# Attention and two MLPs in one kernel: result of attention kept in f32, P transposed in blocks of two chunks by two query tiles, new lags

## The chip, the cores and the metric

The kernel runs on one core of a Trainium2 chip. The metric is the device time of one execution in microseconds (us), as the median of several runs. The engines are TensorE (PE in the rows; PEld is its loading of weights), VectorE (DVE), ScalarE (ACT), GpSimd (POOL) and SyncE (SP), whose queue issues nearly all DMAs.

## The reference

Attention over 4 batches, 8 heads, 576 positions and a head size of 64, with rotary positions on q and k. Its output, 2304 rows of 512, goes through two MLPs in turn. All is float32.

```python
q_rot, k_rot = (rotate(q), rotate(k))
scores = np.matmul(q_rot, k_rot.transpose(0, 1, 3, 2)) / np.sqrt(D)
scores = scores - np.max(scores, axis=-1, keepdims=True)
attn = np.exp(scores)
attn = attn / (np.sum(attn, axis=-1, keepdims=True) + 1e-09)
x = np.matmul(attn, v).transpose(0, 2, 1, 3).reshape(B * S, H * D)
x = (1 / (1 + np.exp(-(x @ w_gate))) * (x @ w_val)) @ w_out      # d_ff 1536
h = x @ w2_in                                                    # d_ff 2048
out = (h * (1 / (1 + np.exp(-1.702 * h)))) @ w2_out
```

## The kernel before

The kernel has an attention stage and an MLP stage. Products that must be nearly exact in f32 are made from numbers split into a high part (the f32 rounded to the type fp32r) and a low part (the rest, rounded likewise): `split_mm` multiplies low by high, high by low and high by high into one PSUM bank.

**Attention.** Work goes by pairs of heads, 16 in all (4 batches x 4 pairs). Of a head's 576 positions 512 are laid out as 4 query tiles of 128 and 64 are a tail. Both tails of a pair share a tile, so a pair has nine score units (`NU`): unit u = 2j + h is query tile j of head h, and unit 8 holds both tails. For each unit TensorE makes the scores (`scores`, L295 and L296), VectorE takes the negated row maximum (L298), ScalarE the exponential with its row sum (`exps`, L313). `normalise` adds 1e-9 to the sums, takes reciprocals (L327, L328) and lets GpSimd scale P in SBUF (L331). P of a query tile (`P`, 128 x 1152 for both heads, 4 buffers) and of the tails (`Pt`, one buffer) is transposed on TensorE in pieces of 128 x 128 (`transpose_p`, L356, L363, L368): three chunks of one query tile go into one PSUM bank (tag `pt`, 3 buffers, which the transposes of q and k share), and one copy on ScalarE or VectorE (L343, L341) takes them to `PT` (one buffer for either half of the queries). `pv` multiplies V by PT (L386: one head in either half of the array's columns, tiles of 128x64; L383: both heads' tails of V in one zero-padded tile that fills the array). One half of a pair's queries (256 columns) and then the other (320) go through the same single PSUM bank (`ps_x`). The result is split at once into `xhl`, high part by ScalarE (L407), low part by VectorE out of PSUM (L409), which is the input of the first MLP.

For the pairs to come, x (q and k) is loaded (L167 to L179), rotated on GpSimd (`rope_mul`, L211, L215) and VectorE (`rope_add`, L219), transposed (`transpose_qk`, L234), split (L243, L244) and stacked by six DMAs on SP's queue (`stack`, L274).

**What sets the order.** The order is written out by hand: `slot(G)` issues, for unit G counted over all pairs, the scores of that unit and whatever is due by tables of lags. `PT` and `PV` give for each transpose step and each P·V step how many units behind the start of its pair it is issued; `ROPE_MUL`, `ROPE_ADD`, `ROPE_T`, `LOAD`, `LOAD_V` how many ahead. `steps` fixes the order in a slot. Every engine works off its own queue in that order, and waits where data or a buffer isn't ready. In pairs 3 to 8 the first weight chunk is loaded and decoded, one instruction per slot (`step_decode`).

**MLPs.** After the last slot the pools of the attention stage are closed and those of the MLP stage opened. Weights come in 14 chunks (6 and 8) of 256 hidden columns; for each chunk all five blocks of rows (four of 512, one of 256) go through `hidden` (L419, `psh`) and `out1` or `out2` (L419, `pso`).

Of the kernel before, what the change touches and what calls it, by code (L numbers as in the profile page):

```python
# [31 lines left out]
def attention_then_mlps(  # L32
# [35 lines left out]
    rp = rot.enter_context(tc.tile_pool(name="rope", bufs=1))  # L68
# [7 lines left out]

    xhl = {}

    def new_xhl(n):
        xhl[n] = big.tile([P, 2, KT, width[n]], F32R, tag=f"xhl{width[n]}", name=f"xhl{n}", bufs=width.count(width[n]))  # L80
# [220 lines left out]
    def exps(i, u):  # L301
# [4 lines left out]
        if h == 0:  # L306
            st[i]["P"][j] = (
                sp.tile([P, 2 * S], F32, tag="P", name="P", bufs=4)
                if j < MAINC
                else sp.tile([P, S], F32, tag="Pt", name="Pt", bufs=1)  # L310
            )
# [21 lines left out]
    PIECES = ((0, 2 * P), (2 * P, S - 2 * P))  # L333


    PT_DVE = ((2, 1), (2, 2), (3, 2), (4, 1))
    PT_DVE_FIRST = ((0, 0), (2, 2), (3, 2))
# [7 lines left out]
    def transpose_p(i, j, g):  # L345


        a = 0 if j < 2 else 1
        if (j, g) in ((0, 0), (2, 0)):
            st[i]["PT", a] = sp.tile([P, NCHK, PIECES[a][1]], F32, tag=f"PT{a}", name=f"PT{a}", bufs=1)  # L350
        PT = st[i]["PT", a]
        pt = st[i]["P"][j]
        ps = ps_t.tile([P, 512], F32, tag="pt", name="ps_p", bufs=3)
        if j < MAINC:
            for t in range(3):
                nc.tensor.transpose(  # L356
                    ps[:, t * P : (t + 1) * P], pt[:, (3 * g + t) * P : (3 * g + t + 1) * P], ident
                )
            jo = (j - 2 * a) * P
            dst = PT[:, 3 * g : 3 * g + 3, jo : jo + P]  # L360
            copy((j, g) in (PT_DVE if i else PT_DVE_FIRST), dst, ps[:, : 3 * P].rearrange("p (t c) -> p t c", t=3))
        elif g == 0:
            nc.tensor.transpose(ps[:TAIL, :P], pt[:, 0:TAIL], ident)  # L363
            for h in range(2):
                copy((j, g) in (PT_DVE if i else PT_DVE_FIRST), PT[h * TAIL : (h + 1) * TAIL, MAINC, 2 * P :], ps[:TAIL, h * TAIL : (h + 1) * TAIL])
        else:
            for t in range(MAINC):
                nc.tensor.transpose(ps[:, t * P : (t + 1) * P], pt[:, TAIL + t * P : TAIL + (t + 1) * P], ident)  # L368
            src = ps.rearrange("p (t h c) -> p h t c", t=MAINC, h=2)
            for h in range(2):  # L370
                t = h * (MAINC + 1)
                copy((j, g) in (PT_DVE if i else PT_DVE_FIRST), PT[:, t : t + MAINC, 2 * P :], src[:, h])

    def pv(i, a, ts):
# [28 lines left out]
        def split():  # L403
            for blk, o, c, w in parts:
                if blk not in xhl:
                    new_xhl(blk)
# [15 lines left out]

    mlp = {}
# [21 lines left out]
    acc = {}  # L445
# [16 lines left out]
    def new_acc(n):  # L462
        acc[n] = mlp["acc"].tile(
            [P, KT * width[n]], F32, tag=f"acc{width[n]}", name=f"acc{n}", bufs=width.count(width[n])
        )

    def out1(c, nchunk, W, n, g):
        if c == 0:
            new_acc(n)
# [3 lines left out]
        for e in range(KT):  # L473
# [7 lines left out]
            if c == nchunk - 1:  # L481
                nc.scalar.activation(xhl[n][:, 0, e, :], a, AF.Copy)
                nc.gpsimd.tensor_tensor(xhl[n][:, 1, e, :], a, f(xhl[n][:, 0, e, :]), ALU.subtract)

    def out2(c, nchunk, W, n, g):
        if c == 0:
            new_acc(n)
# [25 lines left out]
    PT_STEPS = [(j, g) for j in range(MAINC) for g in range(3)] + [(MAINC, 0), (MAINC, 1)]  # L513
# [6 lines left out]
    FILL = 2  # L520
    dec = []
# [21 lines left out]
    def step_normalise(G):  # L543
        for i in range(npairs):
            for j in range(MAINC + 1):
                if G == NU * i + min(2 * j + 2, NU):
                    normalise(i, j)
# [152 lines left out]
```

## Time and profile before

| | us |
|---|---|
| median of 3 runs | 1158.08 |
| lowest, highest | 1157.78, 1158.6 |
| span of the profiled execution | 1156.3 |
| TensorE busy in it | 1125.3 |
| VectorE busy | 753.4 |
| ScalarE busy | 425.7 |
| GpSimd busy | 324.3 |

The span runs from the first to the last instruction of the profiled execution; the profile gives no other time for it. A matmul's duration in the rows is that of one instruction, and matmuls overlap, so what one costs is read from the distance between the starts of two. The attention stage ends, and the MLP stage begins, at 314 us.

### The profile page before, as it was taken

The numbers are of one execution on the slowest core, as the hardware profiler recorded it, in microseconds if no ns is written. First come the engines' busy times: TensorE is split into PE (matmuls) and PEld (weight loads), VectorE is DVE, ScalarE is ACT, GpSimd is POOL, SyncE is SP. The second block draws the span as 40 slices with busy tenths as digits, with TensorE's granted clock in tenths as the row PEclk, the third lists the DMA queues.
The fourth block names the chain that finished last, engine by engine and source line by source line (L and its number), as shares of the span: only waits on it lengthen the run. The fifth ranks groups of instructions, "written<-read, shape, count | busy, mean of one in ns | idle before, by whom it ended". The sixth has DMA issues, their size and how long they took to land.

```text
span 1156.3 us, 16339 instructions
## 1 busy us (share of the span) xinstructions
PE 1125.3 (97%) x6032; PEld 926.1 (80%) x6032; DVE 753.4 (65%) x1467; ACT 425.7 (37%) x937; POOL 324.3 (28%) x335
## 2 busy tenths in 40 slices
PE   3999999999999999999999999999999999999998
PEld 2777777777688888888888888888888888888886
DVE  6788897776454655545555455666767776676744
ACT  3777777777521211221212122342222223232221
POOL 6778787764210100100101002430010010010100
PEclk9999999999999999999999999999999999999999
DMA  4555665544110111111111111111111111111014
GB/s 133 138 145 150 144 165 131 118 100 99 39 53 20 54 38 37 55 37 37 55 37 55 37 37 37 34 39 39 38 46 45 37 55 37 37 55 37 19 37 128
DMA packets 46063, 76.15 MB, mean 66 GB/s; under 512 B 11728, under 2 KB 24016, under 8 KB 45984
## 3 DMA queue, kind: packets, MB, share of 16 engines
q1 hardware_dynamic: 45696, 74.19, 23.9%
q8 instruction: 48, 0.79, 0.3%
q0 software_dynamic: 288, 0.92, 0.2%
q14 instruction: 31, 0.25, 0.1%
HBM read 50.46 MB, written 4.72 MB: 48 GB/s over the span
## 4 chain that ended last, share of the span: by engine, by line
PE 83%; DVE 6%; DMA 5%; SPq 3%; issue 1%; ACT 1%; POOL 0%; POOLq 0%; DVEq 0%; ACTq 0%
PE psh L419 43%; PE pso L419 30%; PE ps_x L386 3%; PE ps_p L356 2%; PE pss L295 2%; DVE xr L219 2%; PE pss L296 2%; DMA Zs<-X 1%; DVE nm L298 1%; DMA X<-Y 1%; SPq L179 1%; DVE Y L244 1%; DVE PT L341 1%; PE ps_x L383 1%; DMA x<-in_k_dram 1%
## 5 line engine op out<-in xcount | busy, mean ns | idle before, releaser
L419 PE MATMUL psh<-xhl,w_in 128*128 128x512 f32 (+1 forms) x2400 | 504.3, 368 | 0.0
L419 PEld LDWEIGHTS psh<-xhl,w_in 128*128 128x128 f32 x2400 | 419.5, 189 | 75.7
L433 ACT ACTIVATE sg<-psh 128x512 f32<-128x512 f32 (+1 forms) x140 | 77.7, 555 | 366.9 <-PE psh L419 366.2
L419 PE MATMUL pso<-w_out,g 128*128 128x512 f32 x864 | 202.4, 389 | 0.0
L435 DVE TENSOR_TENSOR gf<-psh,sg 128x512 f32<-128x512 f32 (+1 forms) x140 | 89.1, 636 | 158.1 <-PE psh L419 111.6
L419 PEld LDWEIGHTS pso<-w_out,g 128*128 128x128 f32 x864 | 161.7, 188 | 33.2
L436 ACT ACTIVATE g<-gf 128x512 fp32r<-128x512 f32 (+1 forms) x140 | 82.5, 589 | 242.5 <-DVE gf L435 242.5
L139 POOL TENSOR_TENSOR w_in<-wt,w_in 128x512 fp32r<-128x512 f32 x40 | 51.8, 1294 | 391.0 <-DVE w_in L138 391.0
L437 DVE TENSOR_TENSOR g<-gf,g 128x512 fp32r<-128x512 f32 (+1 forms) x140 | 95.3, 681 | 91.7 <-ACT g L436 91.7
L419 PE MATMUL pso<-g,w_out 128*128 128x512 f32 (+1 forms) x720 | 152.8, 368 | 0.0
L419 PEld LDWEIGHTS pso<-g,w_out 128*128 128x128 f32 x720 | 125.8, 189 | 22.6
L298 DVE TENSOR_REDUCE nm<-pss 128x1 f32<-128x576 f32 x144 | 107.8, 749 | 52.3 <-PE pss L296 51.2
L331 POOL TENSOR_SCALAR P<-P,r 128x576 f32<-128x576 f32 x128 | 103.9, 824 | 73.2 <-DVE r L328 25.8
L139 POOL TENSOR_TENSOR w_out<-wt,w_out 128x512 fp32r<-128x512 f32 x28 | 36.2, 1293 | 263.9 <-DVE w_out L138 263.9
L313 ACT ACTIVATE P<-pss,nm 128x576 f32<-128x576 f32 x128 | 95.5, 746 | 32.5 <-DVE nm L298 31.8
L495 DVE TENSOR_TENSOR acc<-pso,acc 128x512 f32<-128x512 f32 x126 | 83.2, 686 | 20.3 <-PE pso L419 18.0
L386 PE MATMUL ps_x<-PT,v 128*64 128x320 f32 (+1 forms) x512 | 79.3, 420 | 4.2 <-DVE xhl L409 4.2
L356 PE MATMUL ps_p<-ident,P 128*128 128x128 f32 x576 | 81.7, 273 | 0.9 <-POOL P L331 0.9
L480 DVE TENSOR_TENSOR acc<-pso,acc 128x512 f32<-128x512 f32 (+1 forms) x100 | 61.6, 635 | 28.7 <-PE pso L419 28.7
L343 ACT ACTIVATE PT<-ps_p 128x384 f32<-128x384 f32 (+2 forms) x178 | 71.5, 440 | 21.9 <-PE ps_p L356 21.2
L356 PEld LDWEIGHTS ps_p<-ident,P 128*128 128x128 f32 x576 | 67.9, 140 | 2.2 <-POOL P L331 1.4
L295 PE MATMUL pss<-X 128*128 128x288 f32 (+3 forms) x176 | 54.6, 337 | 1.1 <-ACT P L313 0.5
(62 smaller groups left out, 1034.5 us busy)
## 6 DMA issues: line engine op xcount, KB each, us to landing
raw<-in_moe_w_out_dram SPq DMA_DIRECT2D x28, 512.0 KB, 3.5
raw<-in_moe_w_in_dram SPq DMA_DIRECT2D x16, 512.0 KB, 3.7
raw<-in_moe_w_gate_dram SPq DMA_DIRECT2D x12, 512.0 KB, 3.9
raw<-in_moe_w_val_dram SPq DMA_DIRECT2D x12, 512.0 KB, 3.8
Z<-X SPq DMA_DIRECT2D x15, 288.0 KB, 3.0
Z<-Y SPq DMA_DIRECT2D x15, 288.0 KB, 3.2
X<-Y SPq DMA_DIRECT2D x15, 288.0 KB, 3.1
x<-in_q_dram SPq DMA_DIRECT2D x16, 256.0 KB, 3.1
```

What stands on the lines that cost most here:

```text
L139: lambda: nc.gpsimd.tensor_tensor(w[:, 1, :], f(t), f(w[:, 0, :]), ALU.subtract),
L295: nc.tensor.matmul(ps[:m, n, o : o + w], T[:, q0 : q0 + m], rhs, start=True, stop=False)
L298: nc.vector.tensor_reduce(nm, ps[:, :, :HALF], axis=AX.XY, op=ALU.max, negate=True)
L313: nc.scalar.activation(st[i]["P"][j][:, c : c + S].rearrange("p (n c) -> p n c", n=2), ps[:, :, :HALF], AF.Exp, bias=nm, accum_out=st[i][" ...
L331: nc.gpsimd.tensor_scalar(pt, pt, r[:, c - a : c - a + 1], 1.0, op0=ALU.mult, op1=ALU.mult)
L356: nc.tensor.transpose(ps[:, t * P : (t + 1) * P], pt[:, (3 * g + t) * P : (3 * g + t + 1) * P], ident)
L386: nc.tensor.matmul(ps[h * D : (h + 1) * D, :n], vt[:, h * MAINC + t, :], PT[:, h * (MAINC + 1) + t, :], start=(t == 0), stop=False,)
L419: nc.tensor.matmul(ps, l(sl, a), r(sr, a), start=(sl == 1 and a == 0), stop=(sl + sr == 0 and a == n - 1))
L435: nc.vector.tensor_tensor(gf, pss[-1][:, :wd], sg, ALU.mult)
L436: nc.scalar.activation(g[:, 0, m, :], gf, AF.Copy)
L437: nc.vector.tensor_tensor(g[:, 1, m, :], gf, f(g[:, 0, m, :]), ALU.subtract)
L495: nc.vector.tensor_tensor(a, ps[:, :DM], a, ALU.add)
```

## The change

- The result of P·V is copied to f32 tiles `xf` (ScalarE alone); it is split into `xhl` later, by `split_x`: block 0 at slot 144 + `DRAIN`, the other blocks in the first MLP chunk, one block ahead of `hidden`. `xf` and the accumulators `acc` share buffers; `xhl` lives in pools on the other side of SBUF that are opened where `rot` and `soft` are closed.
- A transpose step takes chunk t and chunk t + 5 of two query tiles: four transposes, one copy of 512 columns; chunk 4 gives two transposes and 256 columns. There are 12 steps per pair where there were 14. The first step of the tails transposes 128 columns of `Pt` where it took 64.
- `normalise` takes two query tiles at once: one add and one reciprocal for four columns. It now comes first in a slot, ahead of the scores.
- Buffers: `P` 5, `Pt` 2, `PT` 2 of each half.
- The lags and the order within a slot are new; which copies go to VectorE (`PT_DVE`) too. Pair 0 has no lags of its own.

```diff
-                nc.scalar.activation(xhl[blk][:, 0, hp, o : o + w], ps[:, c : c + w], AF.Copy)
-            for blk, o, c, w in parts:
-                nc.vector.tensor_tensor(
-                    xhl[blk][:, 1, hp, o : o + w], ps[:, c : c + w], f(xhl[blk][:, 0, hp, o : o + w]), ALU.subtract
-                )
+                at = hp * width[blk] + o
+                nc.scalar.activation(xf[blk][:, at : at + w], ps[:, c : c + w], AF.Copy)
...
+    def split_x(n, e, src, eng):
+        a = src.rearrange("p (e w) -> p e w", w=width[n])[:, e, :]
+        nc.scalar.activation(xhl[n][:, 0, e, :], a, AF.Copy)
+        eng.tensor_tensor(xhl[n][:, 1, e, :], a, f(xhl[n][:, 0, e, :]), ALU.subtract)
+    def split_block(n):
+        new_xhl(n)
+        for e in range(KT):
+            split_x(n, e, xf[n], nc.vector if e % 2 else nc.gpsimd)
...
-    def normalise(i, j):
+    def normalise(i, js):
         s = st[i]["sum"]
-        a = 2 * j
-        b_ = min(a + 2, 2 * MAINC + 1)
-        r = sp.tile([P, 2], F32, tag="r", name="r", bufs=4)[:, : b_ - a]
-        for c in range(a, b_):
-            nc.vector.tensor_scalar_add(r[:, c - a : c - a + 1], s[:, c : c + 1], 1e-9)
+        a = 2 * js[0]
+        b_ = min(2 * js[-1] + 2, NU)
+        r = sp.tile([P, 4], F32, tag="r", name="r", bufs=4)[:, : b_ - a]
+        nc.vector.tensor_scalar_add(r, s[:, a:b_], 1e-9)
         nc.vector.reciprocal(r, r)
         for c in range(a, b_):
-            pt = st[i]["P"][j][:, (c - a) * S : (c - a + 1) * S]
+            j, h = divmod(c, 2)
+            pt = st[i]["P"][j][:, h * S : (h + 1) * S]
             nc.gpsimd.tensor_scalar(pt, pt, r[:, c - a : c - a + 1], 1.0, op0=ALU.mult, op1=ALU.mult)
...
-    PT_DVE = ((2, 1), (2, 2), (3, 2), (4, 1))
+    QT = MAINC + 1
+    PT_DVE = (6, 11, 8, 1, 9, 7)
...
-        if j < MAINC:
-            for t in range(3):
-                nc.tensor.transpose(
-                    ps[:, t * P : (t + 1) * P], pt[:, (3 * g + t) * P : (3 * g + t + 1) * P], ident
-                )
+        if t < QT:
+            chs = (t, QT + t) if t < MAINC else (t,)
+            for x, c in enumerate(chs):
+                for y in range(2):
+                    nc.tensor.transpose(
+                        ps[:, (2 * x + y) * P : (2 * x + y + 1) * P],
+                        st[i]["P"][2 * a + y][:, c * P : (c + 1) * P],
+                        ident,
+                    )
+            dst = PT[:, t : chs[-1] + 1 : QT, : 2 * P]
+            copy(dve, dst, ps[:, : len(chs) * 2 * P].rearrange("p (t c) -> p t c", c=2 * P))
...
-    LOAD, LOAD_V, LOAD_VTAIL = 27, 13, 3
-    ROPE_MUL = {ANY: (20, 19, 16, 17, 18, 15), 1: (22, 20, 18, 14, 17, 14), 2: (22, 20, 17, 22, 18, 17)}
-    ROPE_ADD = {ANY: (15, 10), 1: (15, 14), 2: (13, 11)}
-    ROPE_T = {ANY: (8, 7, 6), 1: (9, 9, 7), 2: (10, 9, 7)}
-    PT = {ANY: (5, 6, 7, 7, 7, 9, 9, 11, 9, 10, 14, 13, 12, 13), 0: (5, 6, 8, 5, 7, 6, 7, 8, 9, 10, 13, 14, 14, 12), npairs - 1: (5, 9, 9, 6, 7, 11, 10, 11, 12, 12, 14, 12, 15, 13)}
+    LOAD, LOAD_V, LOAD_VTAIL = 27, 10, 5
+    ROPE_MUL = {ANY: (24, 20, 19, 18, 24, 13), 1: (21, 19, 19, 18, 19, 16), 2: (21, 19, 13, 20, 20, 19)}
+    ROPE_ADD = {ANY: (11, 10), 1: (16, 10), 2: (11, 12)}
+    ROPE_T = {ANY: (9, 7, 6), 1: (9, 7, 6), 2: (10, 7, 6)}
+    PT_STEPS = [(0, t) for t in range(QT)] + [(1, t) for t in range(QT + 2)]
+    PT = {ANY: (6, 6, 7, 9, 7, 10, 10, 13, 12, 12, 14, 14), npairs - 1: (7, 9, 10, 13, 7, 10, 14, 17, 17, 11, 17, 15)}
+    NORM = ((0, 1), (2, 3), (4,))
-    PV_EARLY = (0, 5, 6, 7, 8, 9)
-    PV = {ANY: (10, 10, 12, 13, 13, 15, 15, 17, 17, 17), 0: (8, 8, 9, 11, 12, 15, 15, 17, 17, 17), npairs - 1: (14, 16, 16, 16, 16, 19, 19, 20, 20, 20)}
+    PV_EARLY = (0,)
+    PV = {ANY: (11, 13, 13, 13, 14, 17, 17, 17, 17, 19), npairs - 1: (11, 16, 16, 16, 16, 21, 22, 22, 23, 23)}
...
-            steps = (step_scores, step_rope, step_decode, run_later, step_pt, step_load, step_pv_early, step_normalise, step_pv, step_exps)
+            steps = (step_normalise, step_scores, step_rope, step_pv, step_decode, step_pv_early, run_later, step_load, step_exps, step_pt)
...
+            if G == NU * npairs + DRAIN:
+                rot.close()
+                mlp["x", 0] = ctx.enter_context(tc.tile_pool(name="xhl_a", bufs=1, side="right", reuse_waits="tile"))
+                split_block(0)
...
+                if at == 0 and n + 1 < NBLK:
+                    split_block(n + 1)
                 g = hidden(kind, W, n)
```

## Rows read from the trace of the kernel before

**Rows 1.** The page: span; busy us (share) xinstructions; granted TensorE clock in 40 slices
```profile
span 1156.3 us, 16339 instructions
...
PE 1125.3 (97%) x6032; PEld 926.1 (80%) x6032; DVE 753.4 (65%) x1467; ACT 425.7 (37%) x937; POOL 324.3 (28%) x335
...
PEclk9999999999999999999999999999999999999999
```

**Rows 2.** Busy time by stretch: a decoding pair, a later pair (stretch, length, engines)
```profile
122.00:140.00 18.00, 17.66 (x131) 13.66 (x129) 15.80 (x42) 13.65 (x37) 15.03 (x17) 1.00 0.61 155
212.00:230.00 18.00, 17.62 (x130) 13.59 (x129) 13.58 (x37) 13.17 (x36) 12.95 (x16) 1.00 0.50 122
```

**Rows 3.** TensorE in order of time, one pair: start, length, line, tiles [idle before]
```profile
200.26 1.08 PE L386 MATMUL ps_x<-PT,v 128*64 128x256 f32 x8
201.27 0.40 PE L295 MATMUL pss<-X 128*128 128x288 f32 x1
201.51 0.30 PE L296 MATMUL pss<-X,Y 128*128 128x288 f32 x1
201.65 0.30 PE L295 MATMUL pss<-X 128*128 128x288 f32 x1
...
203.11 0.49 PE L234 MATMUL ps_qk<-ident,xr 128*128 128x128 f32 x3
203.68 0.27 PE L363 MATMUL ps_p<-ident,Pt 128*64 128x128 f32 x1
203.88 0.65 PE L386 MATMUL ps_x<-PT,v 128*64 128x256 f32 x4
204.46 0.40 PE L295 MATMUL pss<-X 128*128 128x288 f32 x1
...
209.58 1.30 PE L386 MATMUL ps_x<-PT,v 128*64 128x320 f32 x8 [0.29 <-DVE xhl L409]
...
216.01 1.14 PE L356 MATMUL ps_p<-ident,P 128*128 128x128 f32 x9
216.91 0.38 PE L295 MATMUL pss<-Z 128*128 128x288 f32 x1
...
219.29 0.40 PE L295 MATMUL pss<-X 128*128 128x288 f32 x1
```

**Rows 4.** Groups by line and shape: xcount | busy, mean ns | idle before
```profile
L433 ACT ACTIVATE sg<-psh 128x512 f32<-128x512 f32 x112 | 67.1, 599 | 306.4 <-PE psh L419 306.3
...
L493 DVE COPY acc<-pso 128x512 f32<-128x512 f32 x18 | 11.7, 685 | 1.7 <-PE pso L419 1.5
```

**Rows 5.** GpSimd and SP's queue in order of time, from 206 to 226
```profile
210.58 1.47 POOL L331 TENSOR_SCALAR P<-P,r 128x576 f32<-128x576 f32 x2 [0.47 <-DVE r L328]
...
222.53 1.97 POOL L331 TENSOR_SCALAR P<-P,r 128x576 f32<-128x576 f32 x2 [1.31 <-ACT PT L343]
...
214.96 0.39 SPq L187 DMA_DIRECT2D v<-in_v_dram  x1
...
218.71 0.59 SPq L179 DMA_DIRECT2D x<-in_k_dram  x1
```

**Rows 6.** DMA issues, 206 to 226: count, KB each, median us to landing
```profile
x<-in_k_dram SPq DMA_DIRECT2D x2, 16.0 KB, 2.4
```

**Rows 7.** TensorE in order of time, the fill and the start of pair 2
```profile
24.03 0.44 PE L295 MATMUL pss<-X 128*128 128x288 f32 x1
24.27 0.44 PE L296 MATMUL pss<-X,Y 128*128 128x288 f32 x1
...
28.75 0.40 PE L295 MATMUL pss<-Z 128*128 128x288 f32 x1 [0.92 <-ACT P L313]
...
53.08 0.54 PE L295 MATMUL pss<-X 128*128 128x288 f32 x1
```

**Rows 8.** TensorE in order of time, the drain and the first MLP matmul
```profile
311.37 2.38 PE L386 MATMUL ps_x<-PT,v 128*64 128x320 f32 x16 [0.93 <-DVE xhl L409]
...
314.07 6.31 PE L419 MATMUL psh<-xhl,w_in 128*128 128x512 f32 x26
```

More of the change, by code (lines that the diff above doesn't have):

```diff
@@ L67, in attention_then_mlps @@
     ps_t = soft.enter_context(tc.tile_pool(name="ps_t", bufs=1, space=PSUM))
-    rp = rot.enter_context(tc.tile_pool(name="rope", bufs=1))
+    rp = rot.enter_context(tc.tile_pool(name="rope", bufs=1, side="right"))
     ps_s = rot.enter_context(tc.tile_pool(name="ps_s", bufs=2, space=PSUM))
@@ L74, in attention_then_mlps, with new_f32 @@
     vtail = [sp.tile([P, P], F32, tag=f"vtail{n}", name=f"vtail{n}") for n in range(2)]
+    mlp = {}
     xhl = {}
+    xf = {}
+    acc = {}
     def new_xhl(n):
-        xhl[n] = big.tile([P, 2, KT, width[n]], F32R, tag=f"xhl{width[n]}", name=f"xhl{n}", bufs=width.count(width[n]))
+        xhl[n] = mlp["x", min(n, 1)].tile([P, 2, KT, width[n]], F32R, tag=f"xhl{n}", name=f"xhl{n}", bufs=1)
+    def new_f32(n, name):
+        return big.tile(
+            [P, KT * width[n]], F32, tag=f"f32_{width[n]}", name=f"{name}{n}", bufs=width.count(width[n])
+        )
[3 more added lines that the diff above has]
+        eng.tensor_tensor(xhl[n][:, 1, e, :], a, f(xhl[n][:, 0, e, :]), ALU.subtract)
     stage = [stage_a]
@@ L343, in copy, with transpose_p @@
             nc.scalar.activation(dst, src, AF.Copy)
[L345 to L350, printed above, removed]
+    def transpose_p(i, n):
+        a, t = PT_STEPS[n]
+        if ("PT", a) not in st[i]:
+            st[i]["PT", a] = sp.tile([P, 2 * QT - 1 + a, PIECES[a][1]], F32, tag=f"PT{a}", name=f"PT{a}", bufs=2)
         PT = st[i]["PT", a]
-        pt = st[i]["P"][j]
+        dve = n in (PT_DVE if i else PT_DVE_FIRST)
         ps = ps_t.tile([P, 512], F32, tag="pt", name="ps_p", bufs=3)
-        if j < MAINC:
-            for t in range(3):
-                nc.tensor.transpose(
-                    ps[:, t * P : (t + 1) * P], pt[:, (3 * g + t) * P : (3 * g + t + 1) * P], ident
-                )
[L359 to L363, printed above, removed]
+        if t < QT:
[6 more added lines that the diff above has]
+                        ident,
+                    )
+            dst = PT[:, t : chs[-1] + 1 : QT, : 2 * P]
+            copy(dve, dst, ps[:, : len(chs) * 2 * P].rearrange("p (t c) -> p t c", c=2 * P))
+            return
+        pt = st[i]["P"][MAINC]
+        if t == QT:
+            nc.tensor.transpose(ps[:, :P], pt[:, 0:P], ident)
             for h in range(2):
-                copy((j, g) in (PT_DVE if i else PT_DVE_FIRST), PT[h * TAIL : (h + 1) * TAIL, MAINC, 2 * P :], ps[:TAIL, h * TAIL : (h + 1) * TAIL])
+                copy(dve, PT[h * TAIL : (h + 1) * TAIL, MAINC, 2 * P :], ps[:TAIL, h * TAIL : (h + 1) * TAIL])
         else:
@@ L368, in transpose_p @@
                 nc.tensor.transpose(ps[:, t * P : (t + 1) * P], pt[:, TAIL + t * P : TAIL + (t + 1) * P], ident)
[L369 to L372, printed above, removed]
+            dst = PT.rearrange("p (h t) c -> p h t c", h=2)[:, :, :MAINC, 2 * P :]
+            copy(dve, dst, ps.rearrange("p (t h c) -> p h t c", t=MAINC, h=2))
     def pv(i, a, ts):
@@ L404, in split @@
             for blk, o, c, w in parts:
-                if blk not in xhl:
-                    new_xhl(blk)
-                nc.scalar.activation(xhl[blk][:, 0, hp, o : o + w], ps[:, c : c + w], AF.Copy)
-            for blk, o, c, w in parts:
-                nc.vector.tensor_tensor(
-                    xhl[blk][:, 1, hp, o : o + w], ps[:, c : c + w], f(xhl[blk][:, 0, hp, o : o + w]), ALU.subtract
-                )
+                if blk not in xf:
+                    xf[blk] = new_f32(blk, "xf")
+                at = hp * width[blk] + o
+                nc.scalar.activation(xf[blk][:, at : at + w], ps[:, c : c + w], AF.Copy)
         later.append(split)
@@ L443, in hidden @@
         return g
-    acc = {}
     row_runs = []
@@ L460, in attention_then_mlps @@
         row_runs.append(runs)
[L462 to L465, printed above, removed]
     def out1(c, nchunk, W, n, g):
         if c == 0:
-            new_acc(n)
+            acc[n] = new_f32(n, "acc")
         wd = width[n]
@@ L507, in attention_then_mlps @@
     ANY = None
[L508 to L514 removed]
+    LOAD, LOAD_V, LOAD_VTAIL = 27, 10, 5
[5 more added lines that the diff above has]
+    NORM = ((0, 1), (2, 3), (4,))
     PV_STEPS = [(a, [t]) for a in range(2) for t in range(MAINC + 1)]
[L516 to L517 removed]
+    PV_EARLY = (0,)
+    PV = {ANY: (11, 13, 13, 13, 14, 17, 17, 17, 17, 19), npairs - 1: (11, 16, 16, 16, 16, 21, 22, 22, 23, 23)}
     DEC_PAIR, DEC_UNIT = (3, 4)
     FILL = 2
+    DRAIN = 10
     dec = []
@@ L544, in step_normalise @@
         for i in range(npairs):
-            for j in range(MAINC + 1):
-                if G == NU * i + min(2 * j + 2, NU):
-                    normalise(i, j)
+            for js in NORM:
+                if G == NU * i + min(2 * js[-1] + 2, NU):
+                    normalise(i, js)
     def step_rope(G):
```

18 lines of the change are left out of this document (8 added, 10 removed).

## Prediction

> **What bounds the kernel now.** I read the page first: a span of 1156.3 us in which TensorE is busy 97% [rows 1]. That share does not say whether TensorE has anything to give, so the next views are the busy time by stretch and the start times of TensorE's instructions. Of 18 us in the middle of the attention stage TensorE is busy 17.6 while VectorE has 13.6, ScalarE 13.2 and GpSimd 13.0; in the pairs that also decode the first weight chunk the others rise to 15.8, 13.7 and 15.0 [rows 2]. The scores of one unit begin at 201.27 and those of the same unit of the next pair at 219.29 [rows 3]: a pair takes 18.02 us, and the 16 pairs some 288 of the 314 us before the first MLP matmul [rows 8]. The MLPs behind that are untouched but for the splitting of their input, so the question is what of the 18.02 us is work.
>
> Start-to-start differences give it [rows 3]. A score matmul of 288 columns takes 0.135 us (201.51 to 201.65). Nine transposes and the following first score take 0.90 + 0.22 (216.01, 216.91, and the next some 0.22 later), so one transpose takes 0.109. The group of eight P·V matmuls of 256 columns lasts 1.01 to the next score and the group of four 0.58, so one takes (1.01 - 0.58)/4 = 0.107 and, in proportion, 0.133 for 320 columns; the zero-padded tail of V, which fills the array, is twice that each. Per pair: 36 full score matmuls 4.8, the narrow tail unit 0.6, 41 + 9 transposes 5.45, P·V 2.15 + 2.67. That is 15.6 us. The other 2.4 us is what can move.
>
> Where it lies: a group of P·V matmuls (array tiles of 128x64) costs more than its matmuls. Eight of them: 1.01, then 0.24 to the second score instead of 0.135, less 8 x 0.107: 0.25 at the way out. On the way in, the four at 203.88 start 0.20 after a transpose of 0.11: 0.09. I take 0.35 per group; groups of four and of eight give the same, so it goes by group and not by matmul. A pair has five (200.26, 203.88, 209.58 and two more like them): 1.75. The 64-row transpose of the tail starts 0.57 after three transposes of 0.33 (203.11, 203.68): 0.24 lost, and the profile names no releaser; what ends then is the subtraction that frees the PSUM buffer taken three steps before. Last, 0.29 is lost at 209.58 to VectorE's subtraction of the attention result, which holds the one P·V bank. Sum 15.6 + 1.75 + 0.24 + 0.29 = 17.9 of 18.02.
>
> **The change, part by part.** I call the start of a pair's nine units T0, and a unit with all that is issued in it a slot; u is its number in the nine.
>
> Attention result kept in f32. The subtraction on VectorE goes; the one P·V bank is then freed by a single ScalarE copy. With the new lags the tail of the first half lies in u5 and the next use in u8; that of the second half in u1 and the next use in u2, behind score and q/k transposes: some 1.0 us later than the copy is done. The wait of 0.29 goes, and nothing is next in line there. The split returns as four ScalarE copies and four subtractions (two VectorE, two GpSimd) per block: for block 0 in the drain, where these engines have no other work, for the others one block ahead of TensorE in the first MLP chunk, where TensorE is the engine that is busy. I cost it at nothing; uncovered, block 0's chain would cost 4 x 0.6 us on ScalarE [rows 4] plus one subtraction, about 3.3 us, and the last P·V matmuls (3.0 us) and the first low-half matmuls lie over it. In the drain the present kernel waits 0.93 for the same subtraction [rows 8]; that goes too.
>
> New P·V lags. Per pair there are now three groups in 64-column tiles: one step in u2, three in u4, four in u8 directly behind the narrow scores; the two tails of V fill the array and stand alone. Two groups less at 0.35: 0.70 less. Bounds: 0 if the cost goes with something that stays, 0.9 if the way in behind scores (u4) is free as well.
>
> Transposes in twos. The number stays 41; the tail's first one is 128 wide, and moves to u5, where the buffer three steps back has long been copied: 0.24 less. Copies become wider and fewer: 512 columns cost VectorE 0.685 (the copy of an MLP output) and ScalarE 0.60 [rows 4]. VectorE gets five of 512 and one of 256 where it had three of 384 and two of 256, and loses the subtraction and most of nine tiny adds and five reciprocals: within 1 us of 13.6, hence no bound. ScalarE loses a little.
>
> So 0.29 + 0.70 + 0.24 = 1.23 us per pair on TensorE. Against it stand the waits that the trace of before doesn't show, and for these I laid the slots out by hand. TensorE's work in u0 to u8 becomes 1.3, 1.9, 1.6, 1.5, 2.6, 1.5, 1.4, 1.2 and 3.6. It is uneven: u5 to u7 are short, and there the chain score, maximum, exponential is longest against them. Two places come out tight.
>
> First, normalising two tiles at once. The new order puts it ahead of the scores, so VectorE's adds wait for the fourth unit's exponential and the maximum of u4 is queued behind them; u4 begins at T0 + 6.4, and VectorE has from u3, behind a maximum done at 6.1, a q/k split (0.5) and two PT copies (0.65, 0.4) left: to 7.8, with add and reciprocal 8.1. GpSimd then needs four pieces: 0.735 each as a rule, 0.98 where VectorE adds at the same time (two in 1.47 at 210.58, in 1.97 at 222.53 [rows 5]), so T0 + 11.05, and the first transpose step of u6, which reads all four pieces, is asked for at T0 + 11.04 (u6 begins at 10.5, its scores take 0.53). A wait of 0 to 0.2. Ahead of these pieces GpSimd has two rope products in u3 that wait for the new pair's x and for the q/k transposes that free their output. SP issues v at the end of u8 (214.96 before) and the last x piece 3.75 us later (218.71), which lands 2.4 after that [rows 5, 6]: T0 + 6.4; the products end at T0 + 7.5, ahead of 8.1. It just fits.
>
> Second, the three transpose buffers in u7: the fifth step of that run needs the first one's buffer, whose ScalarE copy is queued behind the exponential of u6: maximum to 11.75, exponential to 12.6, copy to 13.15, and TensorE asks at 12.9. About 0.25 of wait. Together I take 0.35 per pair, between 0 and 1.0. Gain 1.23 - 0.35 = 0.88.
>
> The six pairs that decode: one extra VectorE instruction per slot delays nothing on these two chains by my layout, as they run from u5 to u1, and u8 is long. Queues: the stacking DMAs leave in the same slot as before, and v's and x's issue still waits for the last P·V step with v.
>
> Fill. In the first slots TensorE waits for the exponentials (0.92 at 28.75) [rows 7]. P is transposed from unit 6 instead of 5, later steps too; the four pieces are there at about 32.1, the tail unit begins at 34.15; pair 1's q/k come a slot later, and the stacking DMAs then end about 1 us after unit 9 asks, which by my layout begins at 36.4. One pair's slots, 16.65, then put pair 2 at 53.05; before it is 53.08 [rows 7]. But 0.64 us more of work is then outstanding (the second half's tail of V, 0.53, and one transpose).
>
> TensorE's clock in the fill: two scores at 24.03 and 24.27 stand 0.24 us apart [rows 7], 288 columns at the lower level, 1.2 GHz, though the granted clock of that slice reads 9 tenths or more [rows 1]; before that it had mostly waited. In the steady state it is 0.135, the 2.4 level; a first score lasts 0.40 there (201.27) and again at 28.75, against 0.44 at 24.03, so the rate has risen by then, in a stretch full of waits. The Trainium skill (TensorE: Matmul & The Clock Gate, "Part 1: The HAM clock gate") says that low is the default and that activity lifts it. By that rule the thinner slots 1 to 5 could stay at the lower rate. Read from rows alone: five slots x 4 scores x 0.105 = 2.1 us, 2.7 with the q/k transposes, if none of it hides under the exponentials; I put this among the rivals.
>
> Sum: 14 pairs x 0.88 = 12.3, the drain 0.93, the fill 0.03 - 0.64: 12.6 us. The profiled span of 1156.3 becomes 1143.7. The profile gives no time for that execution beside its span; the median of the runs, 1158.1, is 1.8 longer. Adding this, 1145.5.
>
> **The rivals.** No new wait: GpSimd at 0.735 a piece and small reserves where I counted none. 14 x 1.23 + 0.3 = 17.5: 1140.6. For it: the engines other than TensorE have 4 to 5 us free per pair [rows 2].
>
> The P·V cost doesn't go by group (it is paid at each turn between f32 and scores, or the tails of V alone in a slot pay it): 14 x (0.53 - 0.35) + 0.3 = 2.8: 1155.3. For it: no row shows P·V directly behind full-width scores, or a tail of V between scores and transposes.
>
> The fill stays at the lower rate: 1145.5 + 2.7 = 1148.2.
>
> Slower: the new wait on GpSimd outgrows the gain. If x lands 1.5 us later (the lag of the first product behind the load shrinks from seven slots to three), the products end at T0 + 8.7, and with pieces of 0.98 the normalising ends at 12.6: 1.6 us of wait before u6, 1.85 with the second place, against 1.23. 14 x -0.62 + 0.3 = -8.4: 1166.5. It decides from an end of the four pieces at about T0 + 12.1, 1 us later than I work out. Against it: measured landings of x are near 2.4 and the late start would come only with DMA queues fuller than now.
>
> **How the numbers follow.** Forecast 45%, no new wait 18%, cost not by group 14%, slow fill 12%, late normalising 11%. The range takes in all but the last: 1139 to 1157. About 0.2% (2.3 us) is what a measurement of this kernel tells from no change. Faster: the first, second and fourth, and over half of the third, 0.83; same 0.08; slower 0.09.
>
> **What would show it.** A period near 17.15 us from score to score of two pairs; three groups of 128x64 P·V per pair; no wait of P·V for VectorE; a wait of transposes for GpSimd's P of at most 0.2 us and one on a PSUM buffer of about 0.25; pair 2 near 53; the first MLP matmul near 301.5 with no gap. I am wrong if the period stays near 18 (then a new wait stands in u6 or u7, or the group cost is not one), or if the MLP stage itself changes length.

## Result and the profile after

The changed kernel takes 1166.74 us (1166.07 to 1168.45), the kernel before 1158.23 beside it: a ratio of 1.0075, 95% interval 1.0060 to 1.0089. It is slower by 8.5 us; 1145.5 was forecast, and 1157 was the end of the range. The page of the changed kernel, to set beside [rows 1]:

```profile
span 1164.8 us, 15987 instructions
...
PE 1132.9 (97%) x6032; PEld 924.4 (79%) x6032; DVE 779.1 (67%) x1316; ACT 415.9 (36%) x894; POOL 341.4 (29%) x345
...
PEclk9999999999999999999999999999999999999999
```

The instructions of TensorE are as many as before, the granted clock is the same, and TensorE is busy 7.6 us longer. Where that lies is told by four moments in TensorE's order of time, which both kernels have. Attention is divided where the narrow scores of unit 8 start, in pair 1 and in pair 15.

| from ... to | before | after | difference |
|---|---|---|---|
| start to pair 1's narrow scores | 50.77 | 51.96 | +1.2 |
| pair 1's to pair 15's, 14 periods | 250.0 | 241.8 | -8.2 |
| to the first MLP matmul | 13.3 | 13.0 | -0.3 |
| to the end of the span | 842.2 | 858.0 | +15.8 |
| span | 1156.3 | 1164.8 | +8.5 |

So attention became 7.3 us shorter, which has the sign of the forecast, and the MLPs, which were to stay as they were, 15.8 us longer. I take the four parts in the order of their size.

**The MLPs.** TensorE in order of time, a 512 block, the changed kernel (start, length, line, tiles, count):

```profile
530.69 11.38 PE L430 MATMUL psh<-xhl,w_in 128*128 128x512 f32 x48
541.90 3.03 PE L430 MATMUL pso<-g,w_out 128*128 128x256 f32 x24
```

The same block in the kernel before:

```profile
533.31 11.04 PE L419 MATMUL psh<-xhl,w_in 128*128 128x512 f32 x48
544.19 3.04 PE L419 MATMUL pso<-g,w_out 128*128 128x256 f32 x24
```

From the first of 48 first-layer matmuls to the start of what follows them are 11.21 us: 233.5 ns each. Before they are 10.88, 226.7 each. The matmuls don't wait for anybody: the rows name no releaser, and every 512 block of all 14 chunks shows the same. There are 1920 such matmuls (the 2400 of an expectation below takes in those of 256 columns): 1920 x 6.8 ns = 13.1 us, and the second-layer matmuls behind them take 2.0 us more in all (up to nine of each 24, the first ones, stand further apart, the rest 227 ns). Nothing in the code of these matmuls is changed. What is changed is where `xhl` lies: in the compiled program its four 512 blocks started at 128 modulo 512 bytes, like `w_in`; now they hang from the top edge of SBUF on the right side and start at 480, with `w_in` still at 128.

**The pairs.** Busy time by stretch, the changed kernel, to set beside [rows 2]:

```profile
122.00:140.00 18.00, 17.38 (x131) 13.53 (x130) 17.11 (x33) 12.26 (x32) 15.48 (x16) 1.00 0.60 151
212.00:230.00 18.00, 18.00 (x140) 14.05 (x136) 15.13 (x28) 12.88 (x34) 14.05 (x17) 1.00 0.56 126
```

The second row is a pair that doesn't decode: TensorE is busy all 18.00 us. Its order of time there, to set beside [rows 3]:

```profile
210.58 0.20 PE L308 MATMUL pss<-X 128*64 128x64 f32 x1
...
211.26 2.37 PE L400 MATMUL ps_x<-PT,v 128*64 128x320 f32 x16
...
217.86 0.65 PE L400 MATMUL ps_x<-PT,v 128*64 128x256 f32 x4
...
220.68 1.52 PE L400 MATMUL ps_x<-PT,v 128*64 128x256 f32 x12
...
227.40 0.19 PE L308 MATMUL pss<-X 128*64 128x64 f32 x1
```

Three groups of P·V, no idle time in any row, and a period of 16.82. In the first row, a decoding pair, it is 17.97 to 18.25 (17.54 and 17.26 for the first and last of the seven that the decoding touches), hardly less than before: VectorE is busy 17.1 us of it. There TensorE does wait, and the rows tell for what (all three engines of the changed kernel):

```profile
128.50 1.15 DVE L151 CAST w_in<-wt 128x512 fp32r<-128x512 f32 x1
...
137.55 1.25 DVE L147 TENSOR_SCALAR wc<-wc 128x512 f32<-128x512 f32 x1
138.72 0.68 DVE L354 COPY PT<-ps_p 128x512 f32<-128x512 f32 x1
...
137.07 1.44 POOL L228 TENSOR_TENSOR x<-x,cos_sb 128x576 f32<-128x576 f32 x1
138.45 1.00 POOL L224 TENSOR_TENSOR xr<-x,sin_sb 128x288 f32<-128x288 f32 x1
...
139.45 0.44 PE L369 MATMUL ps_p<-ident,P 128*128 128x128 f32 x2 [0.54 <-DVE PT L354]
```

The same two instructions of VectorE in the kernel before (groups by line, two decoding pairs):

```profile
L138 DVE CAST w_in<-wt 128x512 fp32r<-128x512 f32 x2 | 1.3, 626 | 0.0
...
L134 DVE TENSOR_SCALAR wc<-wc 128x512 f32<-128x512 f32 x2 | 0.8, 418 | 0.0
```

VectorE's clamp of the decoded weights takes 1.25 us (0.42 before). It ends at 138.80, 0.3 us after GpSimd's cosine product (137.07 + 1.44); the copy of PT is queued behind it, and the transposes wait for the buffer. In this step TensorE loses 0.7 of the 1.15 us by which the pair is longer than 16.82; the rest comes in delays of 0.2. The cast takes 1.15 (0.63 before) and ends 0.3 us after the cosine product of its time (127.95 + 1.42). The Trainium skill (SBUF — State Buffer, "Who interferes with whom") says that such VectorE instructions may take a port pair that they share with GpSimd, for the whole instruction, and that the second one to come waits; the clamp's row agrees, and a wait of VectorE shows here as a long instruction, not as idle time.

**Fill and start of the MLPs.** TensorE in the fill, to set beside [rows 7]; the last row is the start of pair 2:

```profile
31.41 0.40 PE L308 MATMUL pss<-X 128*128 128x288 f32 x1 [1.26 <-ACT P L326]
...
36.94 0.55 PE L247 MATMUL ps_qk<-ident,xr 128*128 128x128 f32 x3 [0.86 <-DVE xr L232]
37.96 0.37 PE L308 MATMUL pss<-X 128*128 128x288 f32 x1 [0.47 <-ACT PT L356]
...
54.95 0.40 PE L308 MATMUL pss<-X 128*128 128x288 f32 x1
```

And the drain with the first MLP matmuls, to set beside [rows 8], with the splitting of blocks 0 and 1 on VectorE and GpSimd (of the four subtractions in either row two are block 0's):

```profile
304.08 2.37 PE L400 MATMUL ps_x<-PT,v 128*64 128x320 f32 x16
306.38 0.81 PE L397 MATMUL ps_x<-PT,vtail 128*128 128x320 f32 x2
306.78 9.45 PE L430 MATMUL psh<-xhl,w_in 128*128 128x512 f32 x37
...
305.83 6.46 DVE L93 TENSOR_TENSOR xhl<-xf,xhl 128x512 fp32r<-128x512 f32 x4 [0.91 <-ACT xhl L92]
...
305.37 6.38 POOL L93 TENSOR_TENSOR xhl<-xf,xhl 128x512 fp32r<-128x512 f32 x4 [7.07 <-ACT xhl L92]
```

The wait of 0.93 in the drain is gone. Four subtractions take VectorE 6.46 us, 1.6 each, while GpSimd does four of its own; alone, the same one takes 0.68 on VectorE (at 327.33) and 1.28 on GpSimd (e6, below). The first 24 MLP matmuls take 6.26 us from first start to the next group's (5.70 before): the eighth starts at 308.95, where VectorE's second subtraction has just ended (308.90).

### The profile page after: what moved, and what is told of

It is laid out like the page before. It is cut to its first block, busy times and chain, and to the rows that moved or that the text cites. A ratio compares the mean times of both kernels' runs of the same rounds, so it can differ in the third digit from the quotient of the medians.

```text
span 1164.8 us, 15987 instructions
## 1 busy us (share of the span) xinstructions
PE 1132.9 (97%) x6032; PEld 924.4 (79%) x6032; DVE 779.1 (67%) x1316; ACT 415.9 (36%) x894; POOL 341.4 (29%) x345
## 4 chain that ended last, share of the span: by engine, by line
PE 93%; DVE 4%; DMA 1%; ACT 1%; issue 1%; POOL 1%; SPq 0%; POOLq 0%; DVEq 0%; ACTq 0%
PE psh L430 43%; PE pso L430 30%; PE ps_x L400 6%; PE ps_p L369 5%; PE pss L308 4%; PE pss L309 3%; PE ps_x L397 1%; PE ps_qk L247 1%; DVE PT L354 1%; DVE nm L311 1%; PE ps_p L384 1%; DVE wc L147 1%; POOL P L344 0%; DVE xr L232 0%; DMA x<-in_k_dram 0%
## 5 line engine op out<-in xcount | busy, mean ns | idle before, releaser
L430 PE MATMUL psh<-xhl,w_in 128*128 128x512 f32 (+1 forms) x2400 | 518.1, 373 | 0.0
L369 PE MATMUL ps_p<-ident,P 128*128 128x128 f32 x576 | 84.3, 277 | 4.5 <-DVE PT L354 3.1
L369 PEld LDWEIGHTS ps_p<-ident,P 128*128 128x128 f32 x576 | 65.5, 140 | 20.2 <-DVE r L340 5.0
L400 PE MATMUL ps_x<-PT,v 128*64 128x320 f32 (+1 forms) x512 | 72.7, 415 | 0.0
L354 DVE COPY PT<-ps_p 128x512 f32<-128x512 f32 (+1 forms) x93 | 58.5, 643 | 17.4 <-PE ps_p L369 14.8
L224 POOL TENSOR_TENSOR xr<-x,sin_sb 128x288 f32<-128x288 f32 x62 | 53.0, 866 | 18.3 <-PE ps_qk L247 12.9
```

The lines of the kernel that those rows point to most:

```text
L369: nc.tensor.transpose(ps[:, (2 * x + y) * P : (2 * x + y + 1) * P], st[i]["P"][2 * a + y][:, c * P : (c + 1) * P], ident,)
L400: nc.tensor.matmul(ps[h * D : (h + 1) * D, :n], vt[:, h * MAINC + t, :], PT[:, h * (MAINC + 1) + t, :], start=(t == 0), stop=False,)
L430: nc.tensor.matmul(ps, l(sl, a), r(sr, a), start=(sl == 1 and a == 0), stop=(sl + sr == 0 and a == n - 1))
```

## Experiments

### Where the two operands of a matmul lie

The first suspicion was the start of `xhl` itself. e2 takes the kernel before and moves its four 512 blocks by 32 bytes, and what lies behind them by 128:

```diff
+    pad = big.tile([P, 8], F32, name="pad")            # ahead of all
...
+        if "pad2" not in mlp:                          # ahead of w_in
+            mlp["pad2"] = big.tile([P, 24], F32, name="pad2")
```

> The kernel before, with its four 512-wide xhl blocks moved by 32 bytes (a 32-byte tile ahead of them and a 96-byte tile behind them, so that weights and everything else stay at multiples of 64). Theory A: the first-layer matmuls of 512 columns go from 226.7 to about 233.5 ns, total about 1158.2 + 14 = 1172. Rival L: 226.7 ns and 1158, since xhl stays in its region.

Measured: 1173.79 (ratio 1.0132, 1.0117 to 1.0147); first-layer matmuls 234.2 ns apart, attention as before with periods of 18.0. The place of the data alone costs 15 us, with no part of the change made. e1 is the other half of it, the changed kernel with `xhl` moved down by 32 bytes, to 448 modulo 512:

```diff
+    edge = ctx.enter_context(tc.tile_pool(name="edge", bufs=1, side="right"))
+    pad = edge.tile([P, 8], F32, name="pad")
```

> The changed kernel with one unused tile of 32 bytes at the edge of SBUF from which its right-hand pools are laid out, so that the MLPs' input xhl starts 32 bytes lower, at a multiple of 64 bytes; nothing else differs. The changed kernel's first-layer matmuls of 512 columns start 233.5 ns apart where before they stood 226.7 apart, 2400 of them in all, some 14 us. Theory A (the start of the moving operand modulo 64 bytes): 226.7 ns again, total about 1152.5, MLP stage about 842. Rival L (it is the region of SBUF in which xhl now lies, or other engines' traffic to it): 233.5 ns as in the changed kernel, total about 1166.7.

Measured: 1157.21 (0.9989, 0.9979 to 0.9998). Its 48 matmuls:

```profile
526.81 11.17 PE L432 MATMUL psh<-xhl,w_in 128*128 128x512 f32 x48
537.81 3.04 PE L432 MATMUL pso<-g,w_out 128*128 128x256 f32 x24
```

11.00 us, 229.2 ns each: 9.5 us are back, and over a third of the excess per matmul is left, which neither theory had expected. At 384 modulo 512 (e5, below) all of it is gone, 226.7. So far "the start of the streamed operand must be a multiple of 128" fits. e7 tests that from the other side: the kernel before with `xhl` left at 128 and everything behind it moved by 32, `w_in`, `w_out` and `g` among it.

```diff
+        if "pad2" not in mlp:                          # between xhl and w_in
+            mlp["pad2"] = big.tile([P, 8], F32, name="pad2")
```

> The kernel before with xhl's four 512-wide blocks in place and everything behind them, weights and hidden results g among it, moved by 32 bytes. Theory M (what counts is where the streamed operand starts): first-layer matmuls of 512 columns stay at 226.7 ns, those of the second layer, which stream g or w_out, go from 226.7 to about 234: some 1296 of them, 9 us, total about 1168. Rival B (the loaded weights count as well): the first layer slows too, total up to 1181. Rival X (xhl's case was special): 1158.

Measured: 1172.7 (1.0122, 1.0105 to 1.0139).

```profile
538.20 11.36 PE L423 MATMUL psh<-xhl,w_in 128*128 128x512 f32 x48
549.40 2.80 PE L423 MATMUL pso<-g,w_out 128*128 128x256 f32 x22
```

That theory falls. The first-layer matmuls, whose streamed operand is where it was, are slow (11.20 us, 233.3); the second-layer ones, with both `g` and `w_out` at 160 modulo 512, settle at 227; so rival B, slow matmuls in both layers, doesn't hold either. What the slow ones have in common is not a start but a distance: that of the streamed operand from the weights. Two runs tell the two theories apart. e8 is the kernel before with everything moved by 32, so that the distance is 0 again and both starts are 160:

```diff
+    pad = big.tile([P, 8], F32, name="pad")            # ahead of all
```

> The kernel before with one 32-byte tile ahead of everything it keeps in SBUF, so that the first-layer weights and the split input both start at 160 modulo 512 (before: both 128). Theory R, the distance between the two operands' starts decides (a multiple of 128 is free): distance 0, first-layer 512-column matmuls start 226.7 ns apart, time within 0.2% of before, 1158. Theory A, the start of an operand itself decides (32 modulo 64 is dear, whichever operand has it): 233 to 234 ns as in the two kernels with one of them moved, 1172 to 1175.

Measured: 1158.63 (1.0003, 0.9993 to 1.0012).

```profile
533.49 11.04 PE L420 MATMUL psh<-xhl,w_in 128*128 128x512 f32 x48
544.37 3.04 PE L420 MATMUL pso<-g,w_out 128*128 128x256 f32 x24
```

10.88 us, 226.7. e11 is the changed kernel with its left side moved by 96, `w_in` at 224, and `xhl` left at 480, the place at which it was slow:

```diff
+    pad = big.tile([P, 24], F32, name="pad")           # ahead of all, on the left
```

> The changed kernel with one 96-byte tile ahead of everything it keeps on the left side of SBUF: the first-layer weights move to 224 modulo 512, the split input stays at 480, a distance of 256. Theory R (distance a multiple of 128 is free): 226.7 ns between first-layer matmuls, the MLP stage 14 us shorter than in the changed kernel, 1152 to 1153. Theory A (an operand at 32 modulo 64 is dear): both are at 32 modulo 64 here, so 233 ns or more and 1166 to 1167.

Measured: 1151.12 (0.9938, 0.9922 to 0.9955).

```profile
526.42 11.04 PE L431 MATMUL psh<-xhl,w_in 128*128 128x512 f32 x48
537.30 3.04 PE L431 MATMUL pso<-g,w_out 128*128 128x256 f32 x24
```

10.88 us again. Theory R holds in all of the kernels (e6 and e12, at distance 0 as well, have 226.7 too); ns per matmul by start (modulo 512) and distance (modulo 128):

| kernel | `xhl` | `w_in` | distance | ns |
|---|---|---|---|---|
| before | 128 | 128 | 0 | 226.7 |
| e8 | 160 | 160 | 0 | 226.7 |
| e5 | 384 | 128 | 0 | 226.7 |
| e11 | 480 | 224 | 0 | 226.7 |
| e1 | 448 | 128 | 64 | 229.2 |
| e7 | 128 | 160 | 96 | 233.3 |
| after | 480 | 128 | 96 | 233.5 |
| e2 | 160 | 256 | 32 | 234.2 |

The weights of the next matmul are loaded while one streams (a load takes 188 to 189 ns in the rows of all of these), so both operands are read at once. That the two reads disturb each other at some distances is the reading that fits; the runs show the rule, not the circuit. In all of them the weights move together with the rest of their side of SBUF; that the distance is that from the weights, and not from another tile there, is argued: `xhl` and `w_in` are what these matmuls read. The Trainium skill (SBUF — State Buffer, "Who interferes with whom") gives TensorE two independent read ports, one for either operand, and says that it never waits for anyone. The runs differ: with the same instructions and the same other engines, 32 bytes are worth 15 us, and the measurement decides.

Of the 15.6 us between e11 and the changed kernel 15.3 lie in the MLP stage (842.7 us, where it was 858.0): that is the term whole. e11's MLP stage is 0.5 longer than before; that is the start with block 0.

### What slows the decoding pairs

e3 is e1 with the decoding of a piece two slots later, so that the clamp doesn't meet the cosine product.

```diff
-    DEC_PAIR, DEC_UNIT = (3, 4)
+    DEC_PAIR, DEC_UNIT = (3, 6)
```

> e1 with the decode of the first weight chunk started two units later in its pair (unit 6 instead of 4). In the changed kernel the six decoding pairs take 18.0 us where the others take 16.8; VectorE is busy 17.1 of 18 us there, and its clamp takes 1.25 us and its cast 1.15 while GpSimd runs a cosine product, 0.42 and 0.45 otherwise. Theory P (VectorE's SBUF-to-SBUF instructions wait for the GpSimd instruction that runs, and the PT copy behind them is late): the clamp and cast move to other GpSimd work, get shorter, and the decoding pairs fall towards 17.0 to 17.4; total about 1146 to 1149. Rival W (VectorE's plain load bounds these pairs): 18.0 as before, total as e1.

Measured: 1160.66 (1.0018, 1.0008 to 1.0027), 3.4 us above e1, the decoding pairs 18.4 to 18.8, longer by half a microsecond; neither theory had expected that. Groups by line on VectorE, three decoding pairs of e3:

```profile
L234 DVE TENSOR_TENSOR xr<-x,xr 128x576 f32<-128x576 f32 x6 | 6.2, 1038 | 0.0
...
L151 DVE SCALAR_TENSOR_TENSOR wt<-raw,wt 128x512 uint32<-128x512 uint32 x3 | 4.5, 1498 | 0.0
...
L149 DVE TENSOR_SCALAR wc<-wc 128x512 f32<-128x512 f32 x3 | 1.2, 414 | 0.0
```

The clamp is back at 0.41, but another decode instruction now takes 1.50 (0.68 before) and the rotation's add 1.04. Moving one collision made others. So it isn't the one meeting; two theories are left, VectorE's load (V) and GpSimd's one more instruction per pair (G). e9 takes that one away (a copy on ScalarE stands in for GpSimd's subtraction of the low weight part), e10 takes VectorE's five decode instructions away; `xhl` is at 384 in both. Chunk 0's weights are not the reference's in either.

```diff
-                lambda: nc.gpsimd.tensor_tensor(w[:, 1, :], f(t), f(w[:, 0, :]), ALU.subtract),
+                lambda: nc.scalar.activation(w[:, 1, :], f(t), AF.Copy) if first else ...
```

> The changed kernel with the split input at 384 modulo 512, and in the seven decoding pairs GpSimd's subtraction of the low weight part replaced by a copy on ScalarE (the low parts of chunk 0 are then not the reference's); VectorE's five decode instructions stay. Theory V, VectorE's load sets those pairs: their period stays at 17.5 to 18.0 us. Theory G, GpSimd's extra instruction sets them: it falls to 16.8 to 17.1. Pairs that do not decode stay at 16.82 by both. One time: 1151 to 1152 by V, 1145 to 1147 by G.

```diff
+            if first:
+                return [
+                    lambda: nc.scalar.activation(f(c), f(high), AF.Copy, scale=2.0**-112),
+                    lambda: None,                      # x4
+                    lambda: nc.scalar.activation(w[:, 0, :], f(c), AF.Copy),
+                    lambda: nc.gpsimd.tensor_tensor(w[:, 1, :], f(c), f(w[:, 0, :]), ALU.subtract),
+                ]
```

> The changed kernel with the split input at 384 modulo 512, and in the seven decoding pairs VectorE's five decode instructions left out (the scaled high word goes to the split as it is, so chunk 0's weights are not the reference's), the cast on ScalarE, and GpSimd's subtraction kept in its slot. Theory V, VectorE's load sets those pairs: their period falls from 17.97 to 16.8 to 17.0 us, one time 1143 to 1145. Theory G, GpSimd's extra instruction sets them: it stays at 17.5 or more, 1148 to 1150.

Busy time by stretch of a decoding pair, e9 and then e10:

```profile
122.00:140.00 18.00, 17.38 (x129) 13.49 (x130) 17.15 (x32) 12.79 (x33) 14.29 (x15) 1.00 0.63 157
```

```profile
122.00:140.00 18.00, 18.00 (x140) 14.14 (x138) 14.97 (x28) 13.53 (x36) 15.34 (x18) 1.00 0.65 163
```

Without GpSimd's instruction nothing changes: VectorE 17.15, periods of 17.97 to 18.01 (17.57 and 17.27 for the first and last), and one of 19.68. In that one TensorE waits 0.82 for a stacking DMA and 0.73 for VectorE's split of q and k besides the 0.54 for PT; what made those two late stays open. Without VectorE's, TensorE is busy all the time in this stretch, and the seven periods are 16.8 to 17.55, 17.1 in the mean; 1.2 of the 2.0 us by which the seven exceed 16.82 are one wait of 0.7 for a stacking DMA and one of 0.5 for ScalarE's P. So VectorE's decode instructions set those pairs, which is V against G. How much of it is their plain length and how much the waits beside GpSimd's work, e10 doesn't tell: it takes both away. The single times, 1154.28 and 1146.66, lie some 2 us above what was expected of the theory that held: for e9 that is the one period of 19.68, for e10 mostly the seven of 17.1 where 16.9 was expected (1.4).

e5 takes only the cast from VectorE, with `xhl` at 384 modulo 512:

```diff
+    pad = edge.tile([P, 24], F32, name="pad")
...
-                lambda: V.tensor_copy(w[:, 0, :], f(t)),
+                lambda: nc.scalar.activation(w[:, 0, :], f(t), AF.Copy) if first else V.tensor_copy(w[:, 0, :], f(t)),
```

> The changed kernel with 96 unused bytes at the edge of SBUF instead of the 32 of e1 (xhl then starts at 384 modulo 512, a multiple of 128; in e1 it was 448, a multiple of 64 alone, and the 512-column first-layer matmuls stood 229.5 ns apart, still 2.8 above the kernel before, where xhl starts at 128 modulo 512); and with the cast of the decode in the attention stage on ScalarE instead of VectorE. Theory A128 (a multiple of 128 is wanted): 226.7 ns, 5 us less than e1. Rival A64 (64 is all that counts; the rest of the difference is something else): 229.5 as in e1. Separately, theory D (the decoding pairs are bound by VectorE's queue, its waits for GpSimd's instructions included): without the cast, 1.16 us of VectorE per pair, they fall from 18.0 to about 16.9 us, 6 us in all. Rival E (they wait for something else, GpSimd or the buffers): 18.0. Total 1146 with A128 and D, 1151 with D alone, 1157 with neither.

Measured: 1149.78 (0.9926, 0.9911 to 0.9941); decoding pairs 17.74, VectorE 16.5 of 18. Some two tenths per pair for one instruction of five, where theory D had expected 16.9; TensorE still waits 0.5 for VectorE's PT. e12 keeps the work and spreads it: e11 with the cast on ScalarE, a piece in every second pair, its instructions two slots apart.

```diff
-        if dec:
+        if dec and G % 2 == 0:
...
-            if DEC_PAIR <= i < DEC_PAIR + wts[1, 0].n:
+            d, odd = divmod(i - DEC_PAIR, 2)
+            if not odd and 0 <= d < wts[1, 0].n:
```

> The changed kernel with the 96-byte tile ahead of its left side (first-layer matmuls then 226.7 ns apart), the cast of chunk 0's weights on ScalarE, and the decoding of chunk 0 spread: a piece in every second pair from 3 to 13, its instructions two slots apart. Theory V (VectorE's load in a pair sets the slow pairs): VectorE has about 14.1 us per 16.82 us of pair without decoding, and 1.1 to 1.4 more here, so all pairs take 16.85 to 17.1 us instead of six at 17.7 to 18.0: 1144 to 1146. If a decode instruction delays the chain by where it falls, not by the load, twelve pairs take about 17.3: 1149 or more.

Measured: 1149.94 (0.9928, 0.9911 to 0.9944), periods of 17.3 and 16.8 in turn, and one of 18.33. A miss: the load of VectorE is spread (15.05 and 15.99 of 18 in two pairs), but only every second pair gets to 16.8; the others keep 17.3, 0.7 us less than in e11. The waits of TensorE in the stretch 84 to 260 of e12 (for what, total, times, longest) name what is next in line:

```profile
PE ps_p L371 <- POOL P L346: 1.4, 5, 0.3
```

Once VectorE has room, it is GpSimd's P that TensorE waits for, 0.28 at a time. So VectorE sets the pairs as they are; once its load is down, a pair takes 17.3 with VectorE at 16 of 18, and it is the place of the instructions that counts.

### What a group of P·V costs

e4 is e1 with the P·V steps of the first half at 11, 12, 13, 14 and 14, which makes five groups of 128x64 again with the same matmuls:

```diff
-    PV = {ANY: (11, 13, 13, 13, 14, 17, ...
+    PV = {ANY: (11, 12, 13, 14, 14, 17, ...
```

> e1 with the P.V steps of the first half spread over units 3, 4 and 5 instead of all three in unit 4 (the middle pairs alone): five groups of 128x64 tiles per pair as in the kernel before, the same matmuls. Theory G (each group costs 0.35 us of TensorE): the pairs without decoding go from 16.8 to 17.5, 0.70 us for each of nine; in the decoding pairs, which wait for VectorE, less shows; total 6 to 10 us above e1. Rival N (no cost by group, the gain came from the removed waits): period and total as e1.

One period of the narrow scores in order of time, e4:

```profile
229.32 0.19 PE L310 MATMUL pss<-X 128*64 128x64 f32 x1
...
246.70 0.19 PE L310 MATMUL pss<-X 128*64 128x64 f32 x1
```

17.38 against 16.81 in e1: 0.57 for two groups, 0.285 each, with no wait of TensorE in these pairs of either kernel; the time is 1161.91 (1.0029, 1.0017 to 1.0041) against 1157.21, 4.7 more where 6 to 10 were expected. The cost goes by group.

### The best version

e6 puts together what was found: `xhl` at 128 modulo 512, the cast on ScalarE, one more PT copy on ScalarE in the decoding pairs, `DRAIN` 4 and all of block 0's subtractions on GpSimd.

```diff
+    pad = edge.tile([P, 88], F32, name="pad")
...
-            split_x(n, e, xf[n], nc.vector if e % 2 else nc.gpsimd)
+            split_x(n, e, xf[n], nc.vector if e % 2 and n else nc.gpsimd)
```

> The changed kernel with 352 unused bytes (xhl at 128 modulo 512, as in the kernel before), the cast on ScalarE as in e5, in pairs 3 to 9 one PT copy more on ScalarE instead of VectorE, block 0 split six units earlier with all four subtractions on GpSimd. Theory A128: 226.7 ns between 512-column first-layer matmuls; if the first 512 bytes' place itself counts, e5 and e6 differ. Theory D: decoding pairs at 16.8, as the others. The first MLP matmuls wait for nothing (0.5 to 1 us less). Total about 1144; if D fails 1151.

Measured: 1149.47 (0.9924, 0.9909 to 0.9938), faster than both kernels, and 5 above what was expected. The decoding pairs take 17.4 to 17.5 (one 18.49); what TensorE waits for there is now ScalarE's copy of PT, 0.4 at a time. The first 24 MLP matmuls take 5.72 us, as before: the 0.5 at the start of the MLPs was the split with VectorE and GpSimd side by side, or its late start; e6 changes both at once. Most of the gain is that of one tile of 96 bytes in e11; e5, e6 and e12 lie within 0.5 us of each other.

## Why the prediction was wrong

**The step that failed** is in the opening: "The MLPs behind that are untouched but for the splitting of their input". The diff moves `xhl` to another pool on another side of SBUF, which the front section tells and the sum never priced. Where data lies was taken to cost nothing; it cost 15.3 us, more than the whole gain. The last line of what would show it wrong names the case ("if the MLP stage itself changes length"), without a rival for it: the slower rival was worked out for GpSimd's normalising and didn't come, since TensorE waits for nobody in the pairs behind the decoding; that its 1166.5 is so near to what was measured is an accident. Without that term, in e11, the time is 1151.12, inside the range and 5.6 above the forecast. The rest is made of the following.

**Period of a pair.** The three gains were right: the wait for `xhl` and the 64-row transpose's are gone, and two groups fewer are worth 0.57 (taken at 0.70). The 0.35 of new waits was wrong: in pairs that don't decode there is none, and 16.82 is the period of the rival "no new wait" (18.02 - 1.23 = 16.79). That it fits so closely is partly luck: with 0.57 the three gains give 16.92, and of the last 0.1 the runs say nothing. (The terms that the forecast adds to 15.6 make 15.67, which changes nothing.) Seven periods give 7.1 us.

**Decoding pairs.** "One extra VectorE instruction per slot delays nothing" failed. Seven periods give 1.1 us instead of the 6.2 of seven times 0.88. The load outside decoding was estimated well: 15.13 x 16.82 / 18 = 14.1 us per pair, against 13.6 + 1. But the five decode instructions add 2.8 at their lengths in the kernel before, 17.0 in all, and that is more than a pair of 16.82 has; the waits beside GpSimd's work, which make the clamp three times as long, come on top. [Rows 2] had shown 15.8 of 18 there; I read it as room, and did not set it against the shorter period that I was forecasting.

**Fill and drain.** Pair 2 starts at 54.95, forecast 53.05. The slots laid out by hand were 1.2 us late by pair 0's narrow scores (35.34, forecast 34.15), 1.6 by unit 9 (37.96, forecast 36.4), and pair 1 took 17.0 instead of 16.65. The rival's low rate through five slots did not come: two scores stand 0.14 us apart from 27.2 on, in the third slot (from 26.2 on before). The waits in the rows are for exponentials, the rotation and a buffer. How much of it belongs to the change is uncertain: in the other runs with this fill pair 1's narrow scores come at 51.3 to 52.5, in those with the fill of before at 50.8 to 51.7. In the drain the wait of 0.93 is gone as forecast, but eight more P·V matmuls and three more transposes stand behind the last narrow scores, and 0.3 is what is left. Fill and drain together cost 0.9 where 0.3 was to be gained.

**Split of block 0.** Costed at nothing because "these engines have no other work" in the drain; but side by side a subtraction takes VectorE 1.6 us where alone it takes 0.68, and 0.5 us of it lies on TensorE's path.

The sum with the measured sizes: 1.2 - 7.1 - 1.1 - 0.3 + 0.5 + 15.3 = 8.5, the difference of the spans.

## What to carry to other kernels

When a change moves a tensor that TensorE reads to another pool, look up where the compiled program puts it and its weights, and time the untouched matmuls from start to start; if their rate has changed, a pad tile is the first experiment. When a period gets shorter, compare each engine's load in its fullest stretch with the new period, not with the old one. An instruction that is longer than elsewhere and ends shortly after another engine's can be a wait, though the profile shows the engine as busy.

## What was not expected of the hardware

The rate of a 512-column matmul in fp32r depends on the distance between its streamed operand and its weights in SBUF: 226.7 ns at a multiple of 128 bytes, 229.2 at 64 modulo 128, 233.3 to 234.2 at 32 or 96, whatever the starts themselves are. With 256 columns it is 119.8 at a multiple of 128, 117.8 in e1 and 120.0 in the changed kernel: little, and not in the same order.

VectorE's clamp, cast and two-input instructions from SBUF to SBUF took 2 to 3 times as long beside GpSimd's (0.42 to 1.25, 0.63 to 1.15, 0.68 to 1.50).
